# First sequence of a clustered attention: float32 probabilities, turned by TensorE and multiplied on two column halves

## The chip, the core and the metric

The kernel runs on one NeuronCore of a Trainium2 chip: TensorE (PE; its weight loads are listed apart, as PEld), VectorE (DVE), ScalarE (ACT), GpSimd (POOL) and the sync engine (SP), which here issues the DMA transfers. The metric is the device time of one execution in microseconds (us). Lower is better.

## What is computed

Four sequences of 768 tokens go through two stages. The first is attention with 8 heads of 64 values. Queries and keys are each assigned to the nearest of 16 centroids, and a query sees only keys of its own cluster:

```python
mask = q_assign[:, :, :, None] == k_assign[:, :, None, :]
scores = np.where(mask, scale * np.matmul(q, k.transpose(0, 1, 3, 2)), -1000000000.0)
attn = np.exp(scores - np.max(scores, axis=-1, keepdims=True))
attn = attn / (np.sum(attn, axis=-1, keepdims=True) + 1e-09)
x = np.matmul(attn, v)            # (4, 8, 768, 64), then heads side by side: (4, 768, 512)
```

The second takes these rows as `x`: it adds the real part of their two-dimensional Fourier transform, normalizes, and applies a feed-forward layer (512 to 2048 and back, ReLU) with a residual. All inputs and outputs are float32.

## The kernel before

The work goes by sequence, and the second stage of a sequence runs beside the attention of the next. The first sequence's attention therefore has no feed-forward work beside it; what runs beside it is the splitting of the two weight matrices into float16 high and low parts (class `Weights`, lines 713 to 761: ones-matmuls at line 721, joins at 745, halving on ACT, DVE and POOL).

Attention takes the heads in pairs, 16 pairs `pr`, four to a sequence. For each pair `prep` loads queries, keys and values, finds scales, splits queries and keys in float16 parts (465, 466), and makes one-hot cluster codes (487 to 533). Then come six steps `st` of 128 queries. `scores` (539) fills two PSUM tiles `ps_big`, one for each head `j`, of 128 queries by 768 keys: float16 products (550) and a mask product (555). For each head:

- DVE scales the scores, and keeps the row minimum of their negatives (569). In the first sequence it writes into a ring of four float32 tiles that lies in `X[1]`, the rows of the second sequence, which are not in use yet; later it writes back to PSUM.
- ACT makes the exponential (572), then casts it to float16 (580). POOL subtracts the cast from the float32 values (581), which gives a low part.
- A DMA transpose (583, issued by SP) turns high and low parts, 1,536 columns, into `pt`, with keys on the partitions. There are six `pt` buffers.

`attend` (590) multiplies two or three steps later: for each head and each of six blocks of 128 keys three float16 matmuls (601 to 603) with the turned probabilities as weights and the split values `v16` as moving operand; two columns of ones in `v16` give the row sums. The splits of the values are made by `split_v` (429 on ACT, 431 on DVE). After three steps `finish` (607) divides by the sums and writes the rows into `X` (613 to 617).

PSUM holds eight banks: two `ps_big` tiles of two banks each, one bank `ps_o` for `attend`, three banks `ps_f` for everything else. A new `ps_big` tile waits until the tile before the last is read out.

`Overlap.run` places all calls on a list of ticks, with an order number inside a tick: scores of pair `pr`, step `st`, at tick 5 + 6 pr + st with order 1, its attend two ticks later with order 3 (three ticks, as long as 6 pr + st is below LATE = 16). At tick 31 the first sequence is folded (`fold`, line 862) and its transform begins. `Order` then takes the instructions in this program order and simulates the engines with its own price list (`cost`); an engine that is free takes the earliest ready instruction, and PE may take one of the next six groups, if tiles of one kind keep their turn. The resulting order on each engine is fixed.

## Time and profile before

| | us |
|---|---|
| three runs | 1006.6, 1008.78, 1011.18 |
| median | 1008.78 |
| span of the profiled execution | 1003.9 |

The profiled execution's own device time is not listed apart from its span; the median of the runs is 4.9 us above the span. The page gives each engine's busy time as a share of the span. A group of instructions is a line with its engine, operation and tiles; "idle before" is what its engine waited for. "PEclk" or "granted clock" is the share of TensorE's full clock that it was given. In rows by time the columns are start, length, engine, line, operation, tiles (written <- read), shape. In this kernel an instruction's listed length covers latency too, so lengths on one engine can overlap.

### The profile page before, as it was taken

Reading aid. Unit: us, or ns where it says so; the run is one execution under the profiler, and the core shown is the slowest. Engines: PE = TensorE matmul, PEld = TensorE weight load, DVE = VectorE, ACT = ScalarE, POOL = GpSimd, SP = SyncE. Lnnn points to the kernel's source line nnn. Section 1 sums busy time; section 2 is a strip of 40 time slices with the busy share of each in tenths; the row PEclk is TensorE's granted clock in tenths of the full one; section 3 lists DMA queues with packets and bytes.
Section 4 is the critical chain, followed back from the end, with each engine's and each line's share of the span. In section 5 each row is a group of like instructions: output and inputs, shape, how many; then the busy total and the mean of one; then the engine's idle time right before and its main releaser. Section 6 shows DMA issues by size and latency. Waiting matters only on the chain.

```text
span 1003.9 us, 23400 instructions
## 1 busy us (share of the span) xinstructions
PE 895.3 (89%) x9348; PEld 585.2 (58%) x9368; DVE 603.3 (60%) x1276; ACT 605.7 (60%) x948; POOL 595.6 (59%) x702
## 2 busy tenths in 40 slices
PE   3776677677899999989999999899999998899998
PEld 1344434455656758556757567567567584576683
DVE  7878879879556556779665646888454334611110
ACT  6899998766756747558656657567566362342130
POOL 2476667757856746749856557569657371552240
PEclk9889978688899999999999999999999999999999
DMA  7899999998668666699676766787764542311000
GB/s 262 207 238 256 268 254 219 187 167 172 110 129 163 113 148 143 131 163 186 128 164 116 153 115 132 153 174 157 129 127 96 118 94 59 70 26 33 11 11 22
DMA packets 397374, 140.65 MB, mean 140 GB/s; under 512 B 381904, under 2 KB 382928, under 8 KB 397264
## 3 DMA queue, kind: packets, MB, share of 16 engines
q1 hardware_dynamic: 397264, 139.16, 67.3%
q8 instruction: 73, 1.20, 0.5%
q14 instruction: 37, 0.30, 0.1%
HBM read 43.17 MB, written 6.29 MB: 49 GB/s over the span
## 4 chain that ended last, share of the span: by engine, by line
PE 63%; DVE 13%; ACT 8%; DMA 7%; issue 5%; POOL 4%; SPq 0%; ACTq 0%; DVEq 0%; POOLq 0%
PE ps_f L1111 22%; PE ps_f L1081 22%; PE ps_big L550 7%; PE ps_f L931 3%; DMA pt<-ph 2%; DMA pt<-p 2%; PE ps_o L601 2%; PE ps_o L602 2%; PE ps_o L603 2%; DMA scr<-in_q_dram 2%; PE ps_big L555 2%; POOL ph L581 2%; DVE ps_big L569 2%; ACT ph L580 1%; DVE X L569 1%
## 5 line engine op out<-in xcount | busy, mean ns | idle before, releaser
L581 POOL TENSOR_TENSOR ph<-p,ph 128x768 f16<-128x768 f32 x144 | 240.5, 1673 | 132.8 <-ACT ph L580 98.1
L1081 PE MATMUL ps_f<-arena,w1h 128*128 128x256 f16 x1536 | 267.1, 275 | 10.3 <-ACT arena L1089 10.3
L1111 PE MATMUL ps_f<-w2h,arena 128*128 128x512 f16 x768 | 239.7, 380 | 0.2 <-ACT arena L1089 0.2
L1081 PE MATMUL ps_f<-arena,w1l 128*128 128x256 f16 x768 | 210.8, 275 | 0.0
L572 ACT ACTIVATE p<-ps_big,rmx 128x768 f32<-128x768 f32 x144 | 129.6, 901 | 124.3 <-DVE ps_big L569 68.5
L569 DVE TENSOR_SCALAR_CACHE_REDUCE ps_big<-ps_big,sce 128x768 f32<-128x768 f32 x144 | 141.9, 1020 | 80.8 <-PE ps_big L555 77.1
L1111 PEld LDWEIGHTS <-arena 128*128 128x128 f16 x1152 | 109.3, 98 | 125.9 <-issue 5.3
L1090 POOL TENSOR_TENSOR arena<-arena 128x256 f16<-128x256 f32 x192 | 129.7, 683 | 84.5 <-ACT arena L1089 80.7
L1081 PEld LDWEIGHTS <-w1h 128*128 128x128 f16 x1536 | 151.2, 98 | 23.9 <-issue 5.5
L550 PE MATMUL ps_big<-hlk,hlq 64*128 64x384 f16 x1152 | 124.1, 340 | 24.9 <-ACT p L572 16.0
L1111 PE MATMUL ps_f<-w2l,arena 128*128 128x512 f16 x384 | 145.7, 380 | 0.0
L580 ACT CAST ph<-p 128x768 f16<-128x768 f32 x144 | 118.9, 828 | 27.1 <-DMA pt<-ph 26.9
L601 PE MATMUL ps_o<-v,pt 128*128 128x66 f16 x1152 | 122.0, 197 | 11.9 <-DMA pt<-p 7.7
L601 PEld LDWEIGHTS <-pt 128*128 128x128 f16 x1152 | 108.8, 99 | 23.3 <-issue 10.1
L602 PE MATMUL ps_o<-v,pt 128*128 128x64 f16 x1152 | 121.9, 198 | 0.0
L603 PE MATMUL ps_o<-v,pt 128*128 128x66 f16 x1152 | 121.5, 196 | 0.0
L1089 ACT ACTIVATE arena<-ps_f,wrel 128x256 f16<-128x256 f32 x192 | 89.7, 474 | 41.7 <-DVE arena L1086 41.3
L602 PEld LDWEIGHTS <-pt 128*128 128x128 f16 x1152 | 109.2, 99 | 5.2 <-issue 0.8
L603 PEld LDWEIGHTS <-pt 128*128 128x128 f16 x1152 | 109.4, 101 | 0.0
L1086 DVE TENSOR_SCALAR arena<-ps_f,wrel 128x256 f32<-128x256 f32 x96 | 46.2, 481 | 103.9 <-PE ps_f L1081 73.8
L550 PEld LDWEIGHTS <-hlq 64*128 64x128 f16 x1152 | 54.3, 97 | 82.4 <-issue 55.5
L1081 PEld LDWEIGHTS <-w1l 128*128 128x128 f16 x768 | 75.5, 98 | 19.8 <-issue 11.0
(178 smaller groups left out, 1315.3 us busy)
## 6 DMA issues: line engine op xcount, KB each, us to landing
arena<-in_moe_w_ch_dram SPq DMA_DIRECT2D x32, 512.0 KB, 5.1
scr<-in_q_dram SPq DMA_DIRECT2D x16, 384.0 KB, 3.5
scr<-in_k_dram SPq DMA_DIRECT2D x16, 384.0 KB, 4.4
vst<-in_v_dram SPq DMA_DIRECT2D x16, 384.0 KB, 3.8
out_dram<-arena SPq DMA_DIRECT2D x24, 256.0 KB, 2.1
pt<-ph SPq DMA_TRANSPOSE x168, 3.9
arena<-in_cs_dram SPq DMA_DIRECT2D x12, 192.0 KB, 3.7
arena<-in_ss_dram SPq DMA_DIRECT2D x12, 192.0 KB, 3.9
```

The lines of the kernel that those rows point to most:

```text
L550: nc.tensor.matmul(out=ps[j][:, hf, 0:SH], lhsT=hq[rows[j], a, sl], rhs=hk[rows[j], c, hs], start=(i == 0), stop=False)
L569: self.mark = nc.vector.tensor_scalar(out=ju, in0=ps[j][:, :, 0:SH], scalar1=ne, scalar2=None, op0=ALU.mult, op1=ALU.min, accum_out=m)
L572: nc.scalar.activation(x, ju, AF.Exp, bias=m, scale=-1.0)
L580: nc.scalar.copy(out=ph[:, 0], in_=p32)
L581: nc.gpsimd.tensor_tensor(out=ph[:, 1], in0=p32, in1=ph[:, 0], op=ALU.subtract)
L601: nc.tensor.matmul(out=o[:, at:at + W], lhsT=hi, rhs=v16[:, kt, 0:W], start=(kt == 0), stop=False)
L602: nc.tensor.matmul(out=o[:, at:at + D], lhsT=hi, rhs=v16[:, kt, 66:130], start=False, stop=False)
L603: nc.tensor.matmul(out=o[:, at:at + W], lhsT=lo, rhs=v16[:, kt, 0:W], start=False, stop=(kt == ST - 1))
L1081: nc.tensor.matmul(out=ps.rearrange("p (t x) -> p t x", x=P), lhsT=a[:, dc, fs], rhs=c[:, :, dc], start=(i == 0), stop=(i == 11))
L1089: nc.scalar.activation(hh[:, f], ps, AF.Relu, scale=rel[:, f:f + 1])
L1090: nc.gpsimd.tensor_tensor(out=hl[:, f], in0=r, in1=hh[:, f], op=ALU.subtract)
L1111: nc.tensor.matmul(out=ps, lhsT=a[:, f, ts], rhs=c[:, f], start=(i == 0), stop=(i == 47))
```

## The change

For the four pairs of the first sequence (`pr < FIRST`):

- `scores` ends with the exponential, which stays float32 in the ring in `X[1]` and also gives the row sum (`accum_out`). Cast, subtraction and DMA transpose are gone.
- A new function `turn`, one tick later, transposes six blocks of 128 by 128 float32 values for one head with PE into a `ps_big` tile. ACT copies them to a `pt` buffer, which is read as float32; for three of the twelve tiles of a pair DVE copies.
- A new function `attend_first`, two ticks after the scores, multiplies in float32, with the values as weights (64 columns) and the turned probabilities as 128 moving columns. Head 0 writes the partitions 0 to 63 of `ps_o`, head 1 the partitions 64 to 127 (`tile_position`). After three steps the result, which has the head values on the partitions, is copied to SBUF.
- A new function `finish_first` transposes it back with PE in a `ps_f` tile; POOL and DVE prepare the reciprocal sums, and DVE multiplies into `X`.
- The values of the first sequence are not split (`split_v` isn't called); the staged float32 values must live until the pair's last product, so pairs 2 and 3 load them into the buffers that `ph` no longer uses there.
- The planner's price list counts a float32 transpose as 109 ns and another float32 matmul as four cycles a column and 10 ns, without a share for column tiles.

Other sequences keep their path.

```diff
@@ -130,8 +130,10 @@
         n = max([a[3] for a in acc], default=1)
         if e == "PE":
             out, es = [a for a in acc if a[1]][0], [a[4] for a in acc if not a[1]][0]
+            if es == 4:
+                return 109 if getattr(i, "is_transpose", False) else out[3] * 4 / 2.4 + 10
             share = i.tile_size[0] * i.tile_size[1] / P / P if i.tile_size else 1.0
-            return max(out[3] * (4 if es == 4 else 1) / 2.4 + 2.5, 30) * share
+            return max(out[3] / 2.4 + 2.5, 30) * share
         if e == "SP":
             return self.TURN[0] + self.TURN[1] * n if "ranspose" in i.opcode else self.COPY[0]
         a, b = self.LINEAR[e]
@@ -329,11 +331,13 @@
         self.po = Counted(ec(tc.tile_pool(name="ps_o", bufs=1, space=PSUM)), 1, kept)
         self.v16, self.vst, self.vmx, self.nat = {}, {}, {}, {}
         self.hl, self.oht, self.pt, self.otile = {}, {}, {}, {}
+        self.p32, self.sums, self.ot = {}, {}, {}
         self.late, self.centered, self.ready, self.mark = None, False, -1, None
 
     RING = 4
     EX = 1
-    PC = ()
+    FIRST = H // 2
+    EVD = (3, 7, 11)
 
     def psum(self, dt=F32):
         return self.big.tile([P, 1024], dt, name="ps_big")
@@ -413,7 +417,8 @@
     def load_v(self, pr):
         nc, sb = self.nc, self.sb
         b, hp = divmod(pr, H // 2)
-        t = sb.tile([P, 2, S // P * D], F32, name="vst", tag="vst", bufs=2)
+        tag = "ph" if 2 <= pr < self.FIRST else "vst"
+        t = sb.tile([P, 2, S // P * D], F32, name=tag, tag=tag, bufs=2)
         if self.late is not None:
 
             nc.gpsimd.tensor_copy(out=t[:, 0, 0:1], in_=self.late)
@@ -557,11 +562,13 @@
         for j in range(2):
 
             m = sb.tile([P, 1], F32, name="rmx", tag="rmx", bufs=6)
-            early = pr < H // 2
+            early = pr < self.FIRST
             if early:
 
                 n = (2 * st + j) % self.RING * S
                 p32 = self.X[1].rearrange("p a x -> p (a x)")[:, n:n + S]
+                if j == 0 and st % 3 == 0:
+                    self.sums[pr, st // 3] = sb.tile([P, 3, 2, 1], F32, name="rsum", tag="rsum", bufs=2)
             else:
                 p32 = sb.tile([P, S], F32, name="p32", tag="p32", bufs=2)
             x = p32.rearrange("p (h x) -> p h x", h=2)
@@ -569,15 +576,13 @@
             self.mark = nc.vector.tensor_scalar(out=ju, in0=ps[j][:, :, 0:SH], scalar1=ne, scalar2=None, op0=ALU.mult, op1=ALU.min,
                                     accum_out=m)
             self.late = m
+            if early:
+                nc.scalar.activation(x, ju, AF.Exp, bias=m, scale=-1.0, accum_out=self.sums[pr, st // 3][:, st % 3, j])
+                self.p32[pr, st, j] = p32
+                continue
             nc.scalar.activation(x, ju, AF.Exp, bias=m, scale=-1.0)
-            if early and j:
-                ph = sb.tile([P, S], F32, name="p32", tag="p32", bufs=2).bitcast(F16).rearrange("p (a x) -> p a x", a=2)
-            else:
-                ph = sb.tile([P, 2, S], F16, name="ph", tag="ph", bufs=2)
-            if early and j and (st in self.PC):
-                nc.gpsimd.tensor_copy(out=ph[:, 0], in_=p32)
-            else:
-                nc.scalar.copy(out=ph[:, 0], in_=p32)
+            ph = sb.tile([P, 2, S], F16, name="ph", tag="ph", bufs=2)
+            nc.scalar.copy(out=ph[:, 0], in_=p32)
             nc.gpsimd.tensor_tensor(out=ph[:, 1], in0=p32, in1=ph[:, 0], op=ALU.subtract)
             pt = sb.tile([P, 2 * ST, P], F16, name="pt", tag="pt", bufs=PT)
             nc.sync.dma_start(out=pt, in_=ph.rearrange("p a x -> p (a x)"), transpose=True)
@@ -586,6 +591,52 @@
             self.hl.pop(pr)
             self.oht.pop(pr)
 
+
+    def turn(self, pr, st, j):
+
+        nc, p32 = self.nc, self.p32.pop((pr, st, j))
+        ps = self.psum()[:, 0:S]
+        for kt in range(ST):
+            ks = slice(kt * P, (kt + 1) * P)
+            nc.tensor.transpose(out=ps[:, ks], in_=p32[:, ks], identity=self.ident)
+        pt = self.sb.tile([P, 2 * ST, P], F16, name="pt", tag="pt", bufs=PT).rearrange("p a x -> p (a x)").bitcast(F32)
+        if (2 * st + j) in self.EVD:
+            nc.vector.tensor_copy(out=pt, in_=ps)
+        else:
+            nc.scalar.copy(out=pt, in_=ps)
+        self.pt[pr, st, j] = pt
+
+    def attend_first(self, pr, st):
+
+        nc = self.nc
+        if st % 3 == 0:
+            self.otile[pr] = self.po.tile([P, 512], F32, name="ps_o")
+        o = self.otile[pr]
+        pt, v = [self.pt.pop((pr, st, j)) for j in range(2)], self.vst[pr]
+        at = st % 3 * P
+        for kt in range(ST):
+            for j in range(2):
+                nc.tensor.matmul(out=o[D * j:D * (j + 1), at:at + P], lhsT=v[:, j, kt * D:(kt + 1) * D],
+                                 rhs=pt[j][:, kt * P:(kt + 1) * P], start=(kt == 0), stop=(kt == ST - 1),
+                                 tile_position=(0, D * j))
+        if st % 3 == 2:
+            ot = self.ot[pr, st // 3] = self.sb.tile([P, S], F32, name="p32", tag="p32", bufs=2)[:, 0:SH]
+            (nc.vector.tensor_copy if st > 3 else nc.scalar.copy)(out=ot, in_=o[:, 0:SH])
+
+    def finish_first(self, pr, i):
+
+        nc, sb = self.nc, self.sb
+        b, hp = divmod(pr, H // 2)
+        ot, r = self.ot.pop((pr, i)), self.sums.pop((pr, i))
+        ps = self.psf()[:, 0:SH]
+        for t in range(3):
+            ts = slice(t * P, (t + 1) * P)
+            nc.tensor.transpose(out=ps[:, ts], in_=ot[:, ts], identity=self.ident)
+        nc.gpsimd.tensor_scalar(out=r, in0=r, scalar1=1e-9, scalar2=None, op0=ALU.add)
+        nc.vector.reciprocal(out=r, in_=r)
+        x = self.X[b % 2][:, 3 * i:3 * i + 3, hp * P:(hp + 1) * P].rearrange("p s (j d) -> p s j d", j=2)
+        nc.vector.tensor_tensor(out=x, in0=ps.rearrange("p (s j d) -> p s j d", j=2, d=D),
+                                in1=r.broadcast_to([P, 3, 2, D]), op=ALU.mult)
 
     def attend(self, pr, st):
         nc, sb = self.nc, self.sb
@@ -1147,7 +1198,6 @@
     MIX3 = (0, 1, 0, 0, 0, 0, 0, 2, 1, 1)
     F2 = 1
     PIN, PF, PV = (), 29, 1
-    LATE = 16
     CE, WP, WQ = 0.45, 0, 0
 
     def layer(self, b, old):
@@ -1245,11 +1295,21 @@
             t0 = T0 + 6 * pr
             for i, (t, order) in enumerate(self.STEPS if pr else self.STEPS0):
                 at(t0 + t, order, (pinned if i in self.PIN and t0 + t >= self.PF else step) if pr else first, att.prep, pr)
+            early = pr < att.FIRST
             for st in range(ST):
                 at(t0 + st, 1, att.scores, pr, st)
-                at(t0 + st + self.LAG + (6 * pr + st < self.LATE), 3, att.attend, pr, st)
+                if early:
+                    for j in range(2):
+                        at(t0 + st + 1, 0.9 if 6 * pr + st == 6 * att.FIRST - 1 else 2, att.turn, pr, st, j)
+                    at(t0 + st + 2, 3, att.attend_first, pr, st)
+                    if st % 3 == 2:
+                        at(t0 + st + 3 - (6 * pr + st == 6 * att.FIRST - 1), 3.2, att.finish_first, pr, st // 3)
+                else:
+                    at(t0 + st + self.LAG, 3, att.attend, pr, st)
             a, d, e = self.V if pr else self.V0
             at(t0 + a, 7 if pr else 0.1, att.load_v, pr)
+            if early:
+                continue
             at(t0 + d, 4.5, pin if self.PV and t0 + d >= self.PF else call, att.split_v, 2 * pr)
             at(t0 + e, 4.5, pin if self.PV and t0 + e >= self.PF else call, att.split_v, 2 * pr + 1)
         ends = [T0 + 24 * (b + 1) + self.LAG for b in range(B)]
```

## The prediction

> **What bounds the kernel now.** I first read the engines' totals, then cut the span into three stretches at places that the chain of work names: the first scores of sequence 0 (35 us), their end (179 us), the first dense product of the first feed-forward (254 us). Columns of the stretches: length, busy us and instructions of PE, PEld, DVE, ACT, POOL, granted clock, DMA share, GB/s.
>
> ```profile
> PE 895.3 (89%) x9348; PEld 585.2 (58%) x9368; DVE 603.3 (60%) x1276; ACT 605.7 (60%) x948; POOL 595.6 (59%) x702
> 35.00:179.00 144.00, 102.95 (x1295) 59.08 (x1313) 125.09 (x264) 135.15 (x174) 101.52 (x88) 0.87 1.11 241
> 179.00:254.00 75.00, 52.22 (x614) 35.86 (x613) 63.07 (x136) 48.04 (x72) 50.12 (x55) 0.80 0.88 177
> 254.00:1003.00 749.00, 725.13 (x7372) 484.21 (x7371) 389.90 (x806) 400.40 (x675) 437.24 (x521) 0.99 0.57 112
> ```
>
> PE is 89% busy overall, but that is an average of two kernels. From 254 us on it is busy 97% of the time: it is the bound there, and the change touches nothing in that stretch. In the first stretch, the only one that is rewritten, PE is busy 71%, ACT 94%, DVE 87%. So there ACT is the bound and PE has room, 41 us by busy time. The middle stretch has no full engine; it is a chain of hand-overs. Whatever the first two stretches gain or lose passes almost whole to the end.
>
> **What goes.** These rows group the instructions of the first stretch by line (busy us, mean ns, idle before):
>
> ```profile
> L569 DVE TENSOR_SCALAR_CACHE_REDUCE X<-ps_big,sce 128x768 f32<-128x768 f32 x47 | 46.7, 1008 | 7.3 <-PE ps_big L555 5.0 <-POOL ph L581 1.1 <-POOL p L581 1.1
> L572 ACT ACTIVATE X<-X,rmx 128x768 f32<-128x768 f32 x48 | 44.0, 933 | 6.4 <-DVE X L569 6.2
> L581 POOL TENSOR_TENSOR ph<-X,ph 128x768 f16<-128x768 f32 x24 | 39.6, 1650 | 20.7 <-ACT ph L580 16.7 <-DVE ac L509 1.5 <-POOL p L581 1.0
> L581 POOL TENSOR_TENSOR p<-X,p 128x768 f16<-128x768 f32 x23 | 37.9, 1648 | 10.0 <-ACT p L580 6.5 <-issue 1.2 <-POOL w1l L759 0.9
> L580 ACT CAST ph<-X 128x768 f16<-128x768 f32 x24 | 19.8, 824 | 0.8 <-DMA pt<-ph 0.7
> L580 ACT CAST p<-X 128x768 f16<-128x768 f32 x23 | 19.0, 825 | 2.2 <-DMA pt<-p 2.2
> ...
> L583 SPq DMA_TRANSPOSE pt<-ph x24: 1273/1886/2932, 39.6 to 181.2; - x24
> L583 SPq DMA_TRANSPOSE pt<-p x24: 1419/2391/3860, 41.8 to 183.2; - x24
> ```
>
> POOL loses 48 subtractions of 1.65 us, 79 us. SP loses 48 transposes, whose issue holds its queue 24 x 1.9 + 24 x 2.4 = 103 of 144 us. Neither is the bound: ACT idles only 9 us in the stretch, and of that 6.2 us are waits for DVE's minimum and 2.9 us for a transpose that still reads the cast's buffer. So freeing POOL, SP and the DMA engines can return 3 us there, if the copies meet no waits of their own; the room shows in the middle stretch instead. With the casts go the casts and splits of the values (8 on ACT, 8 on DVE).
>
> **ACT's sum.** Durations overlap by some 0.1 us, so I count from start to start (ACT by time; then one line's summary; then groups of the first 300 us, whose 14 value casts and splits are eight of sequence 0 and six later):
>
> ```profile
> 39.12 0.82 ACT L580 CAST p<-X 128x768 f16<-128x768 f32 x1
> 39.84 1.76 ACT L572 ACTIVATE X<-X,rmx 128x768 f32<-128x768 f32 x2
> 41.51 0.82 ACT L580 CAST ph<-X 128x768 f16<-128x768 f32 x1
> ...
> L383 ACT ACTIVATION_READ_ACCUMULATOR X<-X x1: 188/188/188, 2.8 to 2.8; 128x1 f32 x1
> L572 ACT ACTIVATE p<-ps_big,rmx 128x768 f32<-128x768 f32 x26 | 23.4, 900 | 23.6 <-DVE ps_big L569 14.9 <-DVE scp L638 4.5 <-POOL ph L581 2.0
> L429 ACT ACTIVATE v<-vst,scp 128x384 f16<-128x384 f32 x14 | 8.1, 605 | 0.0
> L431 DVE SCALAR_TENSOR_TENSOR v<-vst,scp,v 128x384 f16<-128x384 f32 x14 | 10.7, 785 | 0.0
> ```
>
> A cast holds ACT 0.72 us (39.12 to 39.84), an exponential 0.83. Out: 48 x 0.72 = 34.6 and 8 value casts x 0.5 = 4.0. In: of the 48 turned tiles three in twelve go to DVE, so 36 copies PSUM to SBUF on ACT. No such copy is in the trace; the exponential that reads PSUM takes 900 ns against 933 from SBUF, so I take the cast's 0.72 less 0.03, 0.69 (upper bound 0.80, that exponential): 36 x 0.69 = 24.8. Four copies of 384 columns, 4 x 0.4 = 1.6. The row sum now comes with the exponential, which adds a read of the accumulator; the one in the trace lasts 188 ns. It costs nothing to 0.19 us each; I take 0.09, since ACT's other rows hide 0.1 of their length: 48 x 0.09 = 4.3, ends 0 and 9. ACT: 135.2 - 38.6 + 30.7 = 127, that is -8 us (from -12 to +1 at the ends).
>
> DVE gains 12 copies from PSUM, at most the 1.0 us of L569, which reads the same 768 columns and also scales (I take 0.95, as no bare copy of that size is shown), and four copies of half that size; it loses eight value splits at 0.7, the 0.785 less the overlap: 11.4 + 2 - 5.6 = +8, so 133 of 144 us. POOL and DMA fall far below. Engine sums alone, PE apart, would make the stretch 8 us shorter.
>
> **PE's sum decides.** Rows of PE by time, with the summaries of two lines among them (ns min/median/max):
>
> ```profile
> 102.90 0.19 PE L601 MATMUL ps_o<-v,pt 128*128 128x66 f16 x1
> ...
> 103.96 0.19 PE L603 MATMUL ps_o<-v,pt 128*128 128x66 f16 x1
> 104.08 1.15 PE L550 MATMUL ps_big<-hlk,hlq 64*128 64x384 f16 x12
> 105.16 0.34 PE L555 MATMUL ps_big<-oht 32*128 32x384 bf16 x4
> ...
> 211.97 0.55 PE L501 MATMUL ps_f<-ident,ac 128*128 128x128 f32 x3 [0.26 <-DVE arena L857]
> 212.53 0.49 PE L893 MATMUL ps_f<-ident,arena 128*1 128x128 f32 x3
> L893 PE MATMUL ps_f<-ident,arena x12: 269/271/273, 212.5 to 848.3; 128*1 128x128 f32 x12
> L407 PE MATMUL ps_big<-X x2: 354/364/373, 10.5 to 10.7; 128*128 128x4 f32 x2
> ...
> 107.96 0.45 PE L493 MATMUL ps_f<-hlq,ct 128*32 128x384 f16 x1 [1.91 <-ACT arena L758]
> 107.96 0.48 PE L493 MATMUL ps_f<-hlk,ct 128*32 128x384 f16 x1
> ```
>
> Per step (two heads, 128 queries) the old `attend` is 36 matmuls that last 0.19 us each but start 0.03 apart: 102.90 to 104.08, 1.18 us in all. By their lengths it would be 36 x 0.19 = 6.8; pipelined lengths overlap, so its real price is 24 x 1.18 = 28 us.
>
> New, per step: a float32 pass with 128 moving columns starts every (0.49 - 0.27) / 2 = 0.11 us at the row of L893. Twelve transposes: 1.32. The twelve products are real float32: L407, the only one in the trace, is one call and records two matmuls, so each call is two passes of 128 columns, 0.22, and twelve take **2.64 if they run one after the other, 1.32 if the two column halves run beside each other**. Three more transposes per three steps: 0.11. One after the other the change adds 1.32 + 2.64 + 0.11 - 1.18 = 2.9 us a step, 69 us in 24 steps. The weight loads I count at nothing, as the next one runs under the pass before. L501, which loads 128 columns each time and not one, gives (0.55 - 0.27) / 2 = 0.14; its first matmul follows a wait, so I take 0.11. If every pass took 0.14, it would be 37 x 0.03 x 24 = 26 us more, an end beyond my range.
>
> PE's present 103 us ran at a granted clock of 0.87, 90 us at full clock. 90 + 69 = 159 us of work for a stretch of 144. A denser PE should be granted more (0.99 where it is 97% busy). At that 97% the stretch takes 159 / 0.97 = 164 us: **+20 us**. Ends: +15 with PE without a gap, +29 with clock and density at 0.92 together.
>
> The PSUM buffers say much the same. `ps_big` has two buffers, and each step now fills them four times: both by scores, then both by turned tiles. The next scores need both back. That loop is scores 1.4 (104.08 to 105.5), DVE's two minima 1.9, the second turn 0.66, its copy 0.7, and five hand-overs of some 0.1 to 0.2: 5.4 us. Before, the loop was scores and minima alone, 3.5 us, and a step took 144 / 24 = 6.0. A product of 2.64 between scores and turn outlasts the two minima, and pushes the loop to 1.4 + 2.64 + 1.32 + 0.7 + 0.5 = 6.6 us, 158 us in 24 steps. While a turn waits for a buffer, the later turn and the next scores stand behind it; the products and weight tiles, on other buffers, may pass by the planner's order.
>
> **The middle stretch.** The chain of work there (start, us, what):
>
> ```profile
> 177.80 0.93 ACT X L572
> 184.98 3.79 DMA scr<-in_q_dram
> 191.10 0.56 DVE X L617
> 196.16 3.08 DMA vst<-in_v_dram
> 207.41 4.87 DMA pt<-ph
> 254.55 4.55 PE ps_f L1081 x24
> ```
>
> From the last exponential's end (178.7) to the last write of X (191.7) pass 13 us: cast, subtraction, a transposing DMA, product. The new way is six transposes 0.66, copy 0.7, product 2.64, copy 0.45, three transposes 0.33, product with the reciprocals 0.56 and hand-overs: some 6.5 us. So the fold of sequence 0 may start 6 us sooner: I take **-6**. Nothing if DVE, 84% busy there, holds it; -12 if the loads' 3.8 and 3.1 us and a transpose's 4.9 on this chain, which queue with the old transposes, shrink as well.
>
> The planner's new price of a float32 transpose (109 against 216) can also reorder later work: I take nothing, within the runs' own 4.6 us.
>
> Sum: +20 - 6 = +14 us. The span is 1003.9 us, the median of the runs 1008.8; the 4.9 us around the span stay. **1023 us**, own range 1012 (+15, -12) to 1038 (+29, 0).
>
> **Rivals.** (1) *The column halves run together and ACT stays the bound.* PE then needs 159 - 32 = 127 us of 144 and is covered; ACT gives -8, the middle -6: 995 us (986 to 1003). For it: the float16 matmuls of L493 on column tiles start within 0.01 us of each other (107.96, 107.96). Against it: these are one pass, and here the second pass of a head must follow the first in the same tile, in an in-order queue. The Trainium skill, "TensorEngine Tiling (Array Packing)", section Key Properties, says that different tiles can load weights and multiply in parallel; by that rule this rival holds. The trace agrees for float16 only; no row shows it for float32.
>
> (2) *They run together, but the `ps_big` loop sets the pace.* 5.4 us without queueing; each hand-over to ACT or DVE, 94% and 87% busy with pieces of 0.5 to 1.2 us, costs perhaps 0.3. At 6.2 us a step: 24 x 0.2 = +5, the middle -6: 1008 us (1002 to 1015).
>
> (3) *PE stays slow.* If the granted clock remains at the stretch's 0.87, one after the other: 159 / 0.87 = 183, +39 - 6: 1042 us. It decides from the point where the denser PE isn't granted more. The Trainium skill, "TensorE: Matmul & The Clock Gate", section Part 4: PE-mode transpose, says that transposes don't count as work for the gate. No run here shows that yet; the dense stretch's 0.99 speaks against a clock that stays.
>
> **How the numbers follow.** Forecast 0.44, rival 1 0.33, rival 2 0.18, rival 3 0.05. Range 990 to 1038: it takes most of rival 1, rival 2 and the forecast's own range, and leaves out the tails and rival 3, about 2 in 10. This kernel's measurement tells about 0.5% (5 us) from no change. Slower by more: 0.42 of the forecast's 0.44, 0.04 of rival 2, rival 3: 0.51. Within: 0.02 + 0.12 + 0.02 = 0.16. Faster: 0.31 + 0.02 = 0.33.
>
> **What would show it.** Right: in the first stretch PE near 97% busy at a clock over 0.95, ACT below 85%, the stretch some 164 us long, and the float32 product's 24 matmuls of a step starting 0.11 apart over 2.6 us. Wrong on the product: pairs of starts within 0.02 us and 1.3 us a step, ACT still over 92%. Wrong on the loop: scores that start while a turned tile waits for its copy. The middle is right if the fold starts within 9 us of the last exponential; wrong if the wait moves to DVE.

## The result, and the profile after

Changed: 1021.4 us, median of 4 runs (1020.27 to 1027.06). Before, in the same session: 1009.91 (1006.6 to 1011.18, 4 runs). The ratio is 1.0134, 95% interval 1.0102 to 1.0166: slower by 11.5 us, some 1.3%. The prediction was 1023 us. A few executions that took 1.6 to 3 times as long as all the others (two of the kernel before, one of own_six_dve) are left out of the medians and ratios below.

The time agrees; most of the reason does not. These are the changed kernel's two first stretches and the last one, cut at the same places as before (length, busy us and instructions of PE, PEld, DVE, ACT, POOL, granted clock, DMA share, GB/s):

```profile
35.00:179.00 144.00, 131.46 (x1306) 86.85 (x1306) 118.14 (x256) 124.75 (x201) 28.65 (x45) 0.98 0.37 117
179.00:254.00 75.00, 53.18 (x615) 35.70 (x615) 61.74 (x124) 46.45 (x70) 39.95 (x42) 0.83 0.67 142
254.00:1003.00 749.00, 721.53 (x7351) 484.98 (x7350) 405.64 (x825) 403.36 (x683) 446.70 (x533) 0.99 0.54 114
```

In the first stretch POOL fell from 102 to 29 us and the DMA share from 1.11 to 0.37, as the removed work says. ACT fell from 135 to 125 us, DVE from 125 to 118. PE rose from 103 to 131, at a granted clock of 0.98 in place of 0.87. But no engine is full: PE 91%, ACT 87%, DVE 82%. What sets the pace is no longer one engine's sum.

Three summaries of lines give landmarks (ns min/median/max, then the start of the first and of the last): the exponentials of the first sequence, the folds, of which the first start is the first sequence's, and the dense products. Before, then after:

```profile
L572 ACT ACTIVATE X<-X,rmx x48: 918/932/969, 35.0 to 177.8; 128x768 f32<-128x768 f32 x48
L872 DVE TENSOR_TENSOR arena<-X x8: 1745/1758/3881, 194.3 to 838.5; 128x1536 f32<-128x1536 f32 x8
L1081 PE MATMUL ps_f<-arena,w1h x1536: 269/273/418, 244.3 to 978.5; 128*128 128x256 f16 x192
```
```profile
L580 ACT ACTIVATE X<-X,rmx x48: 918/937/987, 31.2 to 182.7; 128x768 f32<-128x768 f32 x48
L923 DVE TENSOR_TENSOR arena<-X x8: 1751/2290/3185, 205.8 to 854.2; 128x1536 f32<-128x1536 f32 x8
L1132 PE MATMUL ps_f<-arena,w1h x1536: 269/273/421, 253.2 to 994.0; 128*128 128x256 f16 x192
```

| us | before | after | difference |
|---|---|---|---|
| first exponential | 35.0 | 31.2 | -3.8 |
| last exponential | 177.8 | 182.7 | +4.9 |
| fold of the first sequence | 194.3 | 205.8 | +11.5 |
| first dense product | 244.3 | 253.2 | +8.9 |
| end | 1003.9 | 1018.9 | +15.0 |

So the loss has three parts: the first stretch (+4.9 at its end), the hand-over from the last exponential to the fold (16.5 to 23.1 us, +6.6, of which the following transform gives 2.6 back), and +6.1 us in a later part whose code is the same in both kernels. The +15.0 is between two single executions (the one before was a quick one of its kernel, and stands for one order of its instructions; other orders come below); the medians differ by 11.5.

### The profile page after: what moved, and what is told of

Same layout as the page of the kernel before. It is cut to its first block, busy times and chain, and to the rows that moved or that the text cites. A ratio compares the mean times of both kernels' runs of the same rounds, so it can differ in the third digit from the quotient of the medians.

```text
span 1018.9 us, 23251 instructions
## 1 busy us (share of the span) xinstructions
PE 931.1 (91%) x9392; PEld 618.4 (61%) x9392; DVE 612.3 (60%) x1276; ACT 596.1 (59%) x980; POOL 520.7 (51%) x654
## 4 chain that ended last, share of the span: by engine, by line
PE 40%; DVE 6%; POOL 6%; ACT 3%; issue 3%; DMA 2%; SPq 0%; POOLq 0%; DVEq 0%; ACTq 0%
PE ps_f L1132 15%; PE ps_f L1162 15%; PE ps_big L555 3%; POOL ph L586 3%; PE ps_f L982 2%; DVE ps_big L576 1%; ACT p L583 1%; DVE arena L923 1%; DMA pt<-ph 1%; PE ps_o L652 1%; PE ps_o L653 1%; PE ps_o L654 1%; POOL arena L1141 1%; PE ps_big L560 1%; ACT ph L585 1%
## 5 line engine op out<-in xcount | busy, mean ns | idle before, releaser
L586 POOL TENSOR_TENSOR ph<-p,ph 128x768 f16<-128x768 f32 x144 | 240.9, 1675 | 140.3 <-ACT ph L585 89.9
L1132 PE MATMUL ps_f<-arena,w1h 128*128 128x256 f16 x1536 | 268.1, 275 | 10.5 <-ACT arena L1140 8.7
L555 PE MATMUL ps_big<-hlk,hlq 64*128 64x384 f16 x1152 | 120.1, 331 | 20.7 <-ACT p L583 14.4
L652 PE MATMUL ps_o<-v,pt 128*128 128x66 f16 x864 | 86.9, 193 | 1.1 <-DMA pt<-ph 1.1
L653 PE MATMUL ps_o<-v,pt 128*128 128x64 f16 x864 | 86.9, 194 | 0.0
L654 PE MATMUL ps_o<-v,pt 128*128 128x66 f16 x864 | 86.7, 192 | 0.0
L652 PEld LDWEIGHTS <-pt 128*128 128x128 f16 x864 | 79.6, 97 | 6.6 <-issue 1.9
L653 PEld LDWEIGHTS <-pt 128*128 128x128 f16 x864 | 79.5, 97 | 3.8 <-issue 0.3
L654 PEld LDWEIGHTS <-pt 128*128 128x128 f16 x864 | 79.6, 99 | 0.0
```

What stands on the lines that cost most here:

```text
L555: nc.tensor.matmul(out=ps[j][:, hf, 0:SH], lhsT=hq[rows[j], a, sl], rhs=hk[rows[j], c, hs], start=(i == 0), stop=False)
L586: nc.gpsimd.tensor_tensor(out=ph[:, 1], in0=p32, in1=ph[:, 0], op=ALU.subtract)
L652: nc.tensor.matmul(out=o[:, at:at + W], lhsT=hi, rhs=v16[:, kt, 0:W], start=(kt == 0), stop=False)
L653: nc.tensor.matmul(out=o[:, at:at + D], lhsT=hi, rhs=v16[:, kt, 66:130], start=False, stop=False)
L654: nc.tensor.matmul(out=o[:, at:at + W], lhsT=lo, rhs=v16[:, kt, 0:W], start=False, stop=(kt == ST - 1))
L1132: nc.tensor.matmul(out=ps.rearrange("p (t x) -> p t x", x=P), lhsT=a[:, dc, fs], rhs=c[:, :, dc], start=(i == 0), stop=(i == 11))
```

## The first stretch: do the products of two heads run together?

The forecast put twelve float32 products of two passes one after the other, 2.64 us a step; its rival put the two heads beside each other, 1.32. This is PE by time in one step of the changed kernel (start, us):

```profile
86.74 1.31 PE L555 MATMUL ps_big<-hlk,hlq 64*128 64x384 f16 x12
87.99 0.34 PE L560 MATMUL ps_big<-oht 32*128 32x384 bf16 x4
88.26 1.53 PE L619 MATMUL ps_o<-pt,vst 128*64 128x128 f32 x24
89.72 1.54 PE L601 MATMUL ps_big<-ident,X 128*128 128x128 f32 x12
91.10 1.89 PE L772 MATMUL ps_f<-arena 128*128 128x512 bf16 x8
92.92 0.77 PE L555 MATMUL ps_big<-hlk,hlq 64*128 64x384 f16 x3
```

L619 is the product: 24 passes in 1.53 us. With a last pass of 0.27 long, one starts every (1.53 - 0.27) / 23 = 0.055 us, half of a pass's 0.11. The transposes of L601 start (1.54 - 0.27) / 11 = 0.115 apart, which is the pass that the prediction took.

**heads_serial** changes the order of the two loops alone, so that neighbouring passes are of one head, except where the first head's passes give way to the second's:

```diff
-        for kt in range(ST):
-            for j in range(2):
+        for j in range(2):
+            for kt in range(ST):
```

> The changed kernel, with all products of head 0 issued ahead of those of head 1, so that two column halves never work at one time. It should double the float32 product of a step from 1.26 us between first and last start to 2.55. If PE's work set the step as my forecast said (one after the other), the step would grow by 1.3 us and the time by 25 to 31 us. If the ps_big loop sets it, the longer product fits in part beside DVE's two minima (1.9 us): the step grows by 0 to 0.6 us, the time by 0 to 14 us.

Measured: 1029.02 us (4 runs), ratio 1.0206 [1.0172, 1.0240]. Its product by time, the stretch from 60 to 180 us, and its exponentials; behind it the same stretch of the changed kernel:

```profile
117.77 2.46 PE L619 MATMUL ps_o<-pt,vst 128*64 128x128 f32 x24
```
```profile
60.00:180.00 120.00, 116.19 (x1048) 84.39 (x1065) 98.49 (x208) 102.92 (x164) 23.08 (x36) 1.00 0.35 115
```
```profile
L580 ACT ACTIVATE X<-X,rmx x48: 921/935/972, 31.3 to 189.0; 128x768 f32<-128x768 f32 x48
```
```profile
60.00:180.00 120.00, 110.46 (x1119) 72.87 (x1119) 101.95 (x220) 104.47 (x169) 24.13 (x38) 1.00 0.37 118
```

The same 24 passes now take 2.46 us, 0.095 apart on average. That average still holds some overlap: at the change of the head, from 118.70 to 119.08 us, passes of both heads alternate. Cleaner are the last eight passes, all of one head, and twenty passes (ten pairs) from the middle of the changed kernel's product (PE by time, from 119.36 to 120.1 and from 88.59 to 89.505 us):

```profile
119.19 1.04 PE L619 MATMUL ps_o<-pt,vst 128*64 128x128 f32 x8
```
```profile
88.42 1.26 PE L619 MATMUL ps_o<-pt,vst 128*64 128x128 f32 x20
```

One head alone starts a pass every (1.04 - 0.27) / 7 = 0.11 us. Two heads start a pair every (1.26 - 0.27) / 9 = 0.11 us. So in the change as made the halves do run beside each other, and the second adds nothing that these rows show. The Trainium skill, "TensorEngine Tiling (Array Packing)", section Key Properties, says that tiles can multiply in parallel; the trace now agrees for float32 too, 0.11 us for a pair and 0.11 for a single pass.

The second reading is as useful. Made serial, PE is busy 97% of this stretch at full clock: just the picture that the forecast drew. Yet the product's 0.93 us a step more made a step only 0.24 us longer (6.57 us on average from the scores of step 6 to those of step 23, with the rows in the next section, then 6.81). The last exponential came 6.3 us later than in the changed kernel and 11.2 later than before, or 14.9 later if both are counted from the first exponential. So even where the products run mostly one after the other, the stretch grows by the forecast's lower end, +15, and not by its +20.

## What sets the pace of a step

The starts of the scores of steps 0, 6 and 23 in PE by time, before and then after:

```profile
30.55 2.10 PE L550 MATMUL ps_big<-hlk,hlq 64*128 64x384 f16 x12
...
59.07 2.10 PE L550 MATMUL ps_big<-hlk,hlq 64*128 64x384 f16 x12
...
170.16 1.17 PE L550 MATMUL ps_big<-hlk,hlq 64*128 64x384 f16 x12
```
```profile
28.39 1.15 PE L555 MATMUL ps_big<-hlk,hlq 64*128 64x384 f16 x12
...
67.44 1.15 PE L555 MATMUL ps_big<-hlk,hlq 64*128 64x384 f16 x12
...
118.51 0.32 PE L555 MATMUL ps_big<-hlk,hlq 64*128 64x384 f16 x1
119.21 1.13 PE L555 MATMUL ps_big<-hlk,hlq 64*128 64x384 f16 x11 [0.38 <-ACT pt L606]
...
179.11 1.15 PE L555 MATMUL ps_big<-hlk,hlq 64*128 64x384 f16 x12
```

The first six steps took 28.5 us and now take 39.1; the seventeen from step 6 to step 23 took 111.1 and now take 111.7, that is 6.54 and 6.57 each. Between these two executions the loss sits in the first pair: -2.2 (an earlier start) + 10.5 + 0.6 - 4.0 (from the scores of step 23 to the last exponential 7.6 us, now 3.6) = +4.9. Where it sits belongs to this one order of the kernel before, though. price_only, below, has the same instructions in another order: its first six steps took 35.9 us and the seventeen 102.6, 6.0 a step in both. What holds across orders is the end: with three orders of each version the last exponential starts at 176.8 to 180.2 before and at 182.7 to 183.0 now, **4.6 us later in the mean**.

Before, a step followed the last after 3.5 to 7.4 us, with gaps of 10 to 14 about the later changes of the pair, which averaged 6.5 once the stretch was under way: ACT's sum, 94% busy. Now nearly every step takes 5.9 to 7.3 us, from the second pair on with no longer gap at a change of the pair. That is the pace of a loop.

Which loop, the idle time at 119.21 says: after one matmul the scores wait for ACT's copy of a turned tile. In the step shown further above, the next scores (92.92) start 6.18 us after the last (86.74). DVE's minima and ACT's work by time between them:

```profile
88.37 1.02 DVE L576 TENSOR_SCALAR_CACHE_REDUCE X<-ps_big,sce 128x768 f32<-128x768 f32 x1
89.31 1.01 DVE L576 TENSOR_SCALAR_CACHE_REDUCE X<-ps_big,sce 128x768 f32<-128x768 f32 x1
```
```profile
89.97 0.95 ACT L580 ACTIVATE X<-X,rmx 128x768 f32<-128x768 f32 x1
90.80 0.21 ACT L580 ACTIVATION_READ_ACCUMULATOR X<-X,rmx 128x1 f32 x1
90.89 0.94 ACT L580 ACTIVATE X<-X,rmx 128x768 f32<-128x768 f32 x1
...
91.81 1.50 ACT L606 COPY pt<-ps_big 128x768 f32<-128x768 f32 x2
```

This is the `ps_big` loop: two scores fill both buffers, the minima empty them, two turned tiles fill them again, the copies empty them. The first turned tile is written from 89.72, six passes of 0.115, so it is done at about 90.6; its copy starts at 91.81, because two exponentials stand ahead of it on ACT. The scores come after the first copy (91.81 + 0.80) and after PE's other work of L772, which fills the wait. If the copies are what the loop waits for, moving copies from ACT to DVE must shorten a step, and moving them back must lengthen it. Both were run with one more edit, the own output tile, which the next section explains:

```diff
-    EVD = (3, 7, 11)
+    EVD = (1, 3, 5, 7, 9, 11)      # own_six_dve
+    EVD = ()                       # own_none_dve
```

> With the last output's own place, and DVE copies six of a pair's twelve turned tiles (every tile of head 1) in place of three. Theory A (the ps_big loop sets the 6.6 us step; the copy of head 1's tile stands behind two exponentials on ACT): DVE can copy it right after the turn, the step falls by 0.2 to 0.5 us, the last exponential comes 4 to 10 us sooner, the time falls by 3 to 9 us against 1008. Rival B (DVE, 84% busy in the stretch, sets the step): 12 copies of 0.95 us more make the stretch 5 to 11 us longer, the time 1012 to 1019.

> The opposite: with the last output's own place, and ACT copies all turned tiles. Theory A: both copies of a step stand one behind the other on ACT, behind two exponentials; a step in which DVE copied before grows by 0.5 to 0.9 us, 12 steps, so the time rises by 5 to 10 us, to 1013 to 1018. Rival B (DVE sets the step): DVE loses 11 us, the time falls by 3 to 10 us, to 998 to 1005.

Measured: own_six_dve 1006.45 us (9 runs), ratio 0.9988 [0.9971, 1.0006]; own_none_dve 1031.78 (4 runs), 1.0232 [1.0202, 1.0262]. Their exponentials, six then none:

```profile
L580 ACT ACTIVATE X<-X,rmx x48: 919/937/974, 31.7 to 179.6; 128x768 f32<-128x768 f32 x48
```
```profile
L580 ACT ACTIVATE X<-X,rmx x48: 922/937/993, 31.4 to 188.6; 128x768 f32<-128x768 f32 x48
```

A step takes 6.47 us with six copies of a pair on DVE, 6.57 with three, 6.90 with none; the last exponential starts at 179.6, 182.7 (184.1 with the own output tile) and 188.6. From 60 to 180 us the scores' wait for a copy on ACT moves with it (us, times, longest; six, three with the own output tile, none):

```profile
PE ps_big L555 <- ACT pt L606: 1.6, 2, 1.1
```
```profile
PE ps_big L555 <- ACT pt L606: 3.6, 8, 1.0
```
```profile
PE ps_big L555 <- ACT pt L606: 8.9, 17, 1.6
```

So the direction holds at both ends, and in the wait that the loop names, though with six the step fell by only 0.1 us where 0.2 to 0.5 were expected. ACT was busy 99.6, 103.8 and 107.3 of these 120 us, so its sum alone is not the bound. Two limits remain. The copies are ACT's work too, so a shorter wait in the loop and a lighter ACT are not told apart entirely. And PE is busy 92% of this time in the changed kernel, 95% with six copies on DVE, so a faster loop has little left to win. The totals move by more than this stretch does (1031.78 us, where 1013 to 1018 were expected), for a reason that comes below.

The loop can also be cut: the turned tiles can go through `ps_f` in halves of 384 columns, so that `ps_big` carries scores alone.

```diff
-        ps = self.psum()[:, 0:S]
-        for kt in range(ST):
...
+        for hf in range(2):
+            hs = slice(hf * SH, (hf + 1) * SH)
+            ps = self.psf()[:, 0:SH]
+            for kt in range(3):
+                nc.tensor.transpose(out=ps[:, kt * P:(kt + 1) * P], in_=p32[:, hs][:, kt * P:(kt + 1) * P], identity=self.ident)
...
```

> The changed kernel, but tiles are turned through two half-size ps_f buffers each (three banks in rotation) in place of ps_big, copied in halves. Theory A (the two ps_big buffers, filled four times a step, set the 6.6 us step): scores no longer wait for copies, steps shrink to what ACT allows, some 5.6 to 6.0 us, and the last exponential of sequence 0 comes 10 to 20 us sooner; the copy that waits for pair 4's buffers stays late in relation to it, so the time falls by 8 to 16 us. Rival B (PE's work or its clock sets the step): steps stay at 6.4 to 6.8 us and the time within 4 us of 1021. Rival C (ps_f becomes the bound, as weights and preparation use it too): slower than the changed kernel.

Measured: 1045.37 us (4 runs), ratio 1.0369 [1.0331, 1.0407]. Its exponentials, and PE's wait for these copies from 60 to 190 us:

```profile
L580 ACT ACTIVATE X<-X,rmx x48: 920/936/966, 32.8 to 203.5; 128x768 f32<-128x768 f32 x48
```
```profile
PE ps_f L603 <- ACT pt L607: 10.7, 12, 2.9
```

A step takes 7.46 us. The wait for the copy is the same wait in another place: PE now stands at the turn itself (10.7 us), with twice the copies, and the three `ps_f` tiles are also what the weights' splitting and `prep` need. That is the expectation's rival C. So this run doesn't free the loop and can't test it; it shows that a turned tile waits for its copy in `ps_f` too.

## The hand-over to the second stage

The prediction took 6 us off between the last exponential and the fold. Instead 6.6 were added. PE, DVE, POOL and ACT of the changed kernel by time:

```profile
188.75 1.53 PE L619 MATMUL ps_o<-pt,ph 128*64 128x128 f32 x24
...
203.44 0.90 PE L634 MATMUL ps_f<-ident,p 128*128 128x128 f32 x3 [2.63 <-DVE p L624]
```
```profile
200.95 1.03 DVE L576 TENSOR_SCALAR_CACHE_REDUCE ps_big<-ps_big,sce 128x768 f32<-128x768 f32 x1 [3.70 <-PE ps_big L560]
...
202.82 0.56 DVE L624 COPY p<-ps_o 128x384 f32<-128x384 f32 x1
...
204.38 0.56 DVE L638 TENSOR_TENSOR X<-ps_f,rsum 128x384 f32<-128x384 f32 x1
...
205.84 1.75 DVE L923 TENSOR_TENSOR arena<-X 128x1536 f32<-128x1536 f32 x1
```
```profile
199.10 3.23 POOL L586 TENSOR_TENSOR ph<-p,ph 128x768 f16<-128x768 f32 x2 [1.60 <-ACT ph L585]
```
```profile
204.38 0.90 ACT L583 ACTIVATE p<-ps_big,rmx 128x768 f32<-128x768 f32 x1 [1.11 <-PE ps_f L634]
```

The last product ends at 190.28. The copy of its result (L624) comes at 202.82, 12.5 us later. It writes a tile of the tag `p32`, which has two buffers, and by then these are in use by the next sequence: its exponentials go into them and POOL subtracts from them (L586). Of POOL's two subtractions from 199.10 the first ends at 200.7, the second at 202.33. The copy takes the buffer of the first: ACT's exponential at 204.38, the next to write that buffer, waits for PE's transposes of the copied tile (L634). So the copy can't write before 200.7, and DVE idles 3.70 us meanwhile. The last 2.1 us are DVE's own fixed order, in which two minima, from 200.95 to 202.82, stand ahead of the copy. The prediction counted 0.45 us for this copy, and never asked whose buffer it writes.

**ot_own** gives this one copy another home, a tile of the ring in `X[1]` that is free by then:

```diff
-            ot = self.ot[pr, st // 3] = self.sb.tile([P, S], F32, name="p32", tag="p32", bufs=2)[:, 0:SH]
+            if pr == self.FIRST - 1 and st == ST - 1:
+                ot = self.X[1].rearrange("p a x -> p (a x)")[:, 0:SH]
+            else:
+                ot = self.sb.tile([P, S], F32, name="p32", tag="p32", bufs=2)[:, 0:SH]
+            self.ot[pr, st // 3] = ot
```

> Only the last output tile of sequence 0 gets a place of its own (a ring slot of X[1] that is already turned), in place of a buffer of the p32 rotation that pair 4 uses. Theory A (the middle stretch lost time because this copy waits for POOL's subtraction of pair 4's tiles): in the changed kernel the last product ends at 190.3 us and its copy on DVE starts at 202.8, so the copy moves to about 190.5, the fold from 205.8 to about 194, and the time falls by 8 to 12 us, to 1010 to 1013 us. Rival B (the fold is held by DVE's queue or by PE anyway): the copy moves, the fold by less than 3 us, the time stays within 3 us of 1021.

Measured: 1007.88 us (10 runs), ratio 1.0001 [0.9983, 1.0019]. PE and DVE by time:

```profile
190.19 1.53 PE L619 MATMUL ps_o<-pt,ph 128*64 128x128 f32 x24
```
```profile
193.80 0.55 DVE L628 COPY X<-ps_o 128x384 f32<-128x384 f32 x1
...
195.66 0.55 DVE L642 TENSOR_TENSOR X<-ps_f,rsum 128x384 f32<-128x384 f32 x1
...
198.76 1.75 DVE L927 TENSOR_TENSOR arena<-X 128x1536 f32<-128x1536 f32 x1
```

The wait is gone: the copy comes 2.1 us after the product, the fold at 198.8, 7 us sooner (the theory said 194). That shows that the shared buffer made the fold late. It does not show that the whole 13.5 us between the two totals come from it: the first dense product starts at 250.8, only 2.4 us sooner than in the changed kernel. The other 11 us arise later, in code that the edit doesn't touch. Before that is believed to be this edit's gain it needs a test.

**own_act_out** asks whether DVE's queue holds this copy, by giving all output copies to ACT (with the own tile):

```diff
-            (nc.vector.tensor_copy if st > 3 else nc.scalar.copy)(out=ot, in_=o[:, 0:SH])
+            nc.scalar.copy(out=ot, in_=o[:, 0:SH])
```

> With the last output's own place, and ACT in place of DVE for the copies of the output tiles. In the run with the own place the last product ends at 191.7 us and DVE copies at 193.8, since it has splits and minima ahead of it, while ACT idles from 191.3 to 192.5. If DVE's queue is what remains of the wait (theory A), the copy comes 1.5 to 2.5 us sooner, the fold too, the time falls by 1 to 2.5 us. If the fold is held by DVE's other work anyway (rival B): no change beyond 1 us.

Measured: 1022.08 us (4 runs), ratio 1.0148 [1.0116, 1.0179]. The copy ran on ACT at 193.88, no sooner than on DVE, behind ACT's own exponentials and a cast; the fold came at 200.6, the first dense product at 249.3. Up to there it is level with ot_own (250.8), and then it ends 13 us later. So moving the copy from DVE's queue to ACT's wins nothing, and again most of the total is decided where nothing was edited.

## The later part: the plan's order

`Order` plans the whole program, so an edit in the first sequence can move instructions of the last. Three kinds of kernels test what that alone does. **price_only** is the kernel before with the change's new price list and nothing else:

```diff
+            if es == 4:
+                return 109 if getattr(i, "is_transpose", False) else out[3] * 4 / 2.4 + 10
...
```

> The kernel before with nothing but the planner's new price list for float32 matmuls. If new prices reorder later work at a cost (rival, for the 6 us that the changed kernel loses after 254 us), this is 4 to 7 us slower than before. My theory: only 48 transposes and one product are priced anew here, so within 3 us of before (1007 to 1013).

Measured: 1009.02 us (10 runs), ratio 1.0011 [0.9989, 1.0032]. The new prices alone cost nothing that can be told, though they do give another order of the same instructions.

**plan_before_1, plan_after_1, plan_after_2, plan_own_1** keep kernel and prices. They shift only the phase of the windows in which the planner decides whether PE is slow in its model. Every instruction computes the same; only the order on the engines differs (the comments in this excerpt and the next are added here):

```diff
-        self.began, self.clock = {}, (0.0, 0.0, True)
+        self.began, self.clock = {}, (-1000.0, 0.0, True)     # plan_after_2: -2000.0
```

> The kernel before, planner's phase 1 us earlier: shows how far luck of the order alone moves it. Theory A: within 3 us of 1008. Rival B: up to 10 us off, slower rather than faster if the order of before was a good draw.

> The changed kernel with nothing changed but the phase of the clock window in the planner's simulation (1 us earlier). The first 200 us keep almost their order; the order after that differs. Theory A (the wait of the last output tile costs some 12 us and is what makes the changed kernel slower): 1018 to 1024. Rival B (the wait costs only the 2 to 3 us by which the first dense product moved in the run with its own place, and most of the difference is the luck of the later order): the time moves by up to 10 us and may come to 1008 to 1014.

> The same with the phase 2 us earlier. Theory A: 1018 to 1024. Rival B: anywhere from 1008 to 1024.

> The kernel with the last output tile in a place of its own, planner's phase 1 us earlier. Theory A: within 3 us of 1008. Rival B: anywhere from 1005 to 1020.

**graft** joins two plans: the changed kernel's own order up to the first dense product, and from there the order that ot_own has:

```diff
+        cut = began[first]               # first: the first matmul that reads w1h
+        self.graph(own=True)             # last output tile counted as X[1]
+        late, _ = self.schedule()
+        for e in order:
+            head = [x for x in order[e] if began[x] < cut]
+            kept = set(head)
+            order[e] = head + [x for x in late[e] if x not in kept]
...
```

> The changed kernel itself (the last output tile still waits in pair 4's buffers), with its own planned order up to the first dense product of the first feed-forward, and from there the later order that the planner made for the kernel with the place of its own. So the early stretch and the wait are those of the changed kernel, the later order that of the 1008 us run. Theory B (the later order makes most of the difference): 1008 to 1013, the first dense product at 251 to 254 us. Theory A (the wait itself costs some 12 us): 1018 to 1024. Rival C (a later order is good only for the exact state it was planned from): between, 1013 to 1018.

All results, ratios against the runs of the kernel before in the same session; the landmarks are read from the summaries of the same lines as above, in one profiled execution each, which lies up to some 4 us from the median (before in its other sessions: medians of 1007.5 to 1007.95):

| kernel | median us (runs) | ratio, 95% | last exponential | fold | first dense product | from there to the end |
|---|---|---|---|---|---|---|
| before | 1009.91 (4) | | 177.8 | 194.3 | 244.3 | 759.6 |
| price_only | 1009.02 (10) | 1.0011 [0.9989, 1.0032] | 176.8 | 194.7 | 245.6 | 764.7 |
| plan_before_1 | 1013.93 (7) | 1.0057 [1.0032, 1.0081] | 180.2 | 193.0 | 249.7 | 765.7 |
| after | 1021.4 (4) | 1.0134 [1.0102, 1.0166] | 182.7 | 205.8 | 253.2 | 765.7 |
| plan_after_1 | 1022.89 (4) | 1.0149 [1.0110, 1.0188] | 183.0 | 207.3 | 251.7 | 768.2 |
| plan_after_2 | 1025.11 (4) | 1.0172 [1.0132, 1.0211] | 182.8 | 205.9 | 250.5 | 771.4 |
| ot_own | 1007.88 (10) | 1.0001 [0.9983, 1.0019] | 184.1 | 198.8 | 250.8 | 755.8 |
| plan_own_1 | 1023.64 (4) | 1.0153 [1.0116, 1.0190] | 183.5 | 199.7 | 248.8 | 775.0 |
| graft | 1018.61 (5) | 1.0111 [1.0092, 1.0129] | 182.5 | 205.6 | 252.9 | 763.2 |

ot_own and plan_own_1 are the same instructions in two orders. The summaries of the dense products, ot_own then plan_own_1:

```profile
L1136 PE MATMUL ps_f<-arena,w1h x1536: 269/273/422, 250.8 to 981.8; 128*128 128x256 f16 x192
```
```profile
L1136 PE MATMUL ps_f<-arena,w1h x1536: 269/273/421, 248.8 to 999.0; 128*128 128x256 f16 x192
```

plan_own_1 begins this part 2.0 us sooner and starts its last product 17.2 us later. Length and number of the products are the same; only how they stand in line differs. PE is busy 731 us of this part in ot_own and 737 in plan_own_1, and idle 24 and 38: the scores' waits for an exponential, for one, grew from 1.3 to 10.2 us. The medians lie 15.8 us apart. So **ot_own's 1007.88 was mostly a lucky order**, not the worth of its edit: by the first dense product the own tile gains some 2 us (250.8 and 248.8, mean 249.8, against 253.2, 251.7 and 250.5, mean 251.8; single executions, and the two sets overlap). graft, with the changed kernel's start and ot_own's later order, missed the 1008 to 1013 of its theory B: its later part lies between the two (763.2 against 765.7 and 755.8). Its 1018.61 would fit theory A, by which the wait costs the time; but plan_own_1, which hasn't that wait, is slower still, and above both of its own expected ranges. So the later order carries over in part only, perhaps because it was made for a fold that comes 7 us sooner; no run tests that.

Is the change's own +11.5 then luck as well? Not all of it. Against the kernel before in the same session, three orders of it give 1, 1.0011 and 1.0057, mean 1.0023; three of the changed kernel 1.0134, 1.0149 and 1.0172, mean 1.0152. The two sets don't touch. At the fold the means are 194.0 and 206.3 us, +12.3. The transform behind it gives 7 of these back, and at the first dense product the means are 246.5 and 251.8, +5.3; that part belongs to the rewritten stretches. The rest, some +5 in the mean of the later part (763.3 and 768.4), lies inside what an order alone does (755.8 to 775.0), so **whether it is systematic stays open** with three orders of each.

No version clearly beats the kernel before. own_six_dve is the lowest at 0.9988 [0.9971, 1.0006], which is no difference; and it is one draw of the order, as ot_own was.

## Why the prediction came out near, point by point

- **"2.64 if they run one after the other"**: the step that failed. The two halves run beside each other: 1.53 us for 24 passes, 2.46 when made serial. The sum of PE's work was over by about 24 x 1.1 us = 26; without them it is 133 us, and PE is no longer the bound of a stretch of 144. This is the condition of rival 1, held at 0.33 and set behind the forecast with the argument that the second pass of a head must follow the first in an in-order queue. It need not stand still: the pass of the other head starts beside it.
- **The first stretch, "+20 us"**: the last exponential came 4.9 us later, after a start 3.8 sooner. PE was 91% busy and not 97%, ACT 87% and not below 85%. Against rival 1, though, ACT's smaller sum (125 us between the fixed cuts, where 127 was predicted) gave no shorter stretch, so ACT's sum isn't the bound either.
- **Rival 2, "the `ps_big` loop sets the pace", 6.2 us a step**: nearest in its mechanism for this stretch, with 6.57 us a step. That its +5 is close to the +4.9 found is luck: the steps cost +11.1, and an earlier start and a shorter end gave 6.2 back. The 6.0 us that it took for a step before is an average that hides 4.8 in the first pair and 6.5 later in one order, and fits price_only's. Moving the copies moved the step in both directions; a hand-over costs more than the 0.3 assumed where two exponentials stand ahead of a copy (90.6 to 91.81). The sign set for a wrong loop, scores that start while a turned tile waits, was not seen in the steps shown, but for one first matmul (118.51) while the second tile was being copied.
- **The middle, "-6"**: wrong in sign, +6.6 at the fold, by one buffer. The durations of the sum were off one by one, but not together: product 1.53 for 2.64, copy 0.56 for 0.45, transposes 0.90 for 0.33 (from 195.1 to 208.5 us the granted clock was 0.50; in ot_own the transposes took 0.55). What it left out was the wait for the tile that the copy writes. "Wrong if the wait moves to DVE" was nearest: the wait sits at a DVE instruction, but 10.4 of its 12.5 us come from a buffer that POOL still reads. The transform behind it took 47.4 us and not 50.0 to the first dense product; ot_own, 7 us sooner at the fold, was only 2.4 sooner there.
- **"The planner's new price ... I take nothing"**: right for the prices (1.0011), wrong for what it stood for. A new order alone moved one kernel by 15.8 us, so "the runs' own 4.6 us" was no bound for it.
- **The 4.9 us around the span**: it is 1.75 (1020.65 for the execution with the span of 1018.9). The profiled execution of before was one of the quick ones, and the rest of the 4.9 was the distance to the median.
- **Clock, copies, accumulator**: as priced. The stretch got 0.98, so rival 3 is out; a copy of 768 columns lasts 0.80 us on ACT (0.70 from start to start) and 0.95 on DVE in the rows below; an accumulator read adds 0.09 (90.80 to 90.89) to an exponential's pitch.

```profile
L606 ACT COPY pt<-ps_big 128x768 f32<-128x768 f32 x36 | 27.5, 798 | 0.5 <-PE ps_big L601 0.5
...
L604 DVE COPY pt<-ps_big 128x768 f32<-128x768 f32 x12 | 11.4, 951 | 2.6 <-PE ps_big L601 2.3
```

So +14 was +20 - 6, and what happened, in the means of three orders, was +4.6 at the end of the first stretch, +5.3 by the first dense product, and some +5 in a later part that may be the order alone. That the sums are alike is chance.

## What to carry to other kernels

When no engine's sum fills a stretch, time the loop of its scarcest buffer, with the queue ahead of each reader, before trusting any sum. For every result that a change writes, ask whose buffer it is and who still reads it. In a kernel whose order is planned as a whole, compare several orders of each version: here one code spans 15.8 us, more than the change itself.

## What the hardware showed that was not expected

Float32 products on two column halves run fully beside each other, two passes each: a pair starts every 0.11 us, as one pass alone does, provided that neighbouring passes belong to different halves. PE held a granted clock of 0.98 from 35 to 179 us, where float32 transposes are 36.5 of its 131.5 busy us; the Trainium skill, "TensorE: Matmul & The Clock Gate", section Part 4: PE-mode transpose, says that these don't count as busy in the same way. Nothing of that is seen here: the other 95 us are less than the 103 for which the kernel before was granted 0.87. But no run holds transposes alone, so this is not shown for them by themselves. The float32 transposes start 0.115 us apart on average in these rows.
